# Two attention and two feed-forward layers on one core: tile statistics issued one tile ahead, the first K steps on two transposed chunks, the fourth tile transposed by DMA, the denominator's halves stacked in one operand

## The chip, the core and the metric

The kernel runs on one core of a Trainium2 chip (trn2). The metric is the device time of one execution in microseconds (us); lower is better. One profiled execution gives the rows that are quoted here. Its engines are named as in the profile: PE (TensorE matmuls), PEld (TensorE weight loads), DVE (VectorE), ACT (ScalarE), POOL (GpSimd) and SP (SyncE, which here only issues DMAs).

## The reference

x has 2048 rows of 1024 bf16 numbers. Four layers follow each other, attention and feed-forward in turn, each with a layer norm and a residual. Cut to what matters:

```python
def _A_ref(x, wqkv, wo):              # linear attention, 32 heads of 32
    q, k, v = split(x @ wqkv)
    phi = lambda t: jnp.where(t > 0, t + 1, jnp.exp(t)) + 1e-6
    pq, pk = phi(q), phi(k)
    kv = jnp.einsum("bhsd,bhse->bhde", pk, v)
    z = jnp.einsum("bhsd->bhd", pk)                       # sum over all rows
    num = jnp.einsum("bhqd,bhde->bhqe", pq, kv)
    den = jnp.einsum("bhqd,bhd->bhq", pq, z)[..., None] + 1e-6
    return merge(num / den) @ wo

def _B_ref(x, w_gate, w_up, w_down):  # width 3584
    return ((x @ w_gate) * (x @ w_up)) @ w_down

x = x + _A_ref(_layernorm(x), ...); x = x + _B_ref(_layernorm(x), ...)
x = x + _A_ref(_layernorm(x), ...); x = x + _B_ref(_layernorm(x), ...)
```

## The kernel before

The 2048 rows are 16 tiles of 128 rows; four tiles are a group. x stays in SBUF (`X`). The order of instructions on each engine is the order in which the kernel's code calls them: there is no scheduler, and each engine works through its own list and waits where a semaphore is not there yet. All DMAs are issued by SP, in the order of the code. They use eight semaphores in turn, so that the ninth DMA is issued only when the first has landed, and so on.

**Layer A** (attention, `layer_A`, L221) goes through these stages.

- *Norm and transpose.* `ln_stats(t)` (L180) takes mean and variance of a tile on DVE (two statistics instructions, L183, and an aggregate, L185) and has POOL form rstd, the inverse standard deviation (L187, L189). `ln_apply(t)` (L192, row L194) writes the normalized tile `XN`. `turn` (L197) transposes a tile into `xT` by DMA; `norm(t)` (L337) is all three.
- *The first group of the first layer* is different (L348 to L399). Nothing is there to be computed while x comes in, so the first tiles are only centred (`centre`, L349, x minus mean), and PE transposes them by multiplying with an identity (`turn_pe`, L354, eight 128x128 chunks into one PSUM tile). ACT copies chunks 0 to 3 to `xT` (L361), DVE chunks 4 to 7 (`turn_rest`, L363, row L364). The factor rstd is applied later, as a scale of the activations. The mean of tile 1 comes from ACT (L372). `idle(n)` (L172) are n matmuls on zeros. `k_part(t, a, b)` (L230) does the steps a to b of the K product of tile t, two 128x512 matmuls for each step (`both`, L202, row L204); step k needs row block k of the K weights, which come in eight DMAs of 256 KB.
- *K and Q.* `k_unit` and `q_unit` are 16 matmuls each. `phi` (L206) follows: ACT makes exp and relu (L209, L210), DVE finishes (L213, L214). `weave` puts one DVE job of the list `fill` after each unit of the list `main`. In the first layer these are the norm steps of the tiles 4 to 15 and then `zs`, additions of finished K tiles to the f32 accumulator `zacc` (`z_unit`, L255, row L258).
- *z.* `zacc` holds one sum for each partition. `z_split` (L261) divides it into two bf16 halves: the rounded value (L262) and the rest (L263). `z_sum` (L265) multiplies both with a matrix of ones, which adds up the 128 partitions and puts the sum on all of them, and ACT copies it back to `zacc` (L269).
- *Products.* `g_unit(m)` (L286) is 32 matmuls over all tiles of `XN` and K; the 31st needs K of tile 15. ACT copies its result (L291). `kv_unit(m)` (L296) is eight 128x128 matmuls (L301). `div_unit(t)` (L271) divides Q by the denominator on DVE (L276 to L282) and has it transposed by DMA. `q_with_m` (L310) and `out_unit` (L328) end the layer. L423 to L428 give the order: two g units, then `z_sum`, `kv_unit(0)`, and so on.

**Layer B** (feed-forward) is `gu_unit` (L452) and `d_unit` (L472) for each group. For the very last tile, `d_end` (L481) replaces `d_unit`: it cuts the 1024 output columns into pieces of 512, 256 and 256, with 28 matmuls for each; every piece is added to `X` (L468) and stored (L470).

PSUM gives three buffers to the tag `mm` (1024 f32 a partition) and one to `kv`.

Of the kernel before, what the change touches and what calls it, by code (L numbers as in the profile page):

```python
# [9 lines left out]
ALU = mybir.AluOpType  # L10
AX = mybir.AxisListType
BF16 = mybir.dt.bfloat16
F32 = mybir.dt.float32
# [13 lines left out]
def kernel(  # L27
# [11 lines left out]
    nc = tc.nc  # L39
    P = 128  # L40
    S, D = A_x.shape[1], A_x.shape[2]
    F = B_w_gate.shape[1]
    NT = S // P
    KD = D // P
# [3 lines left out]
    TPG = G // P  # L48
# [7 lines left out]
    small = ctx.enter_context(tc.tile_pool(name="small", bufs=4))  # L56
    psum = ctx.enter_context(tc.tile_pool(name="psum", bufs=1, space=bass.MemoryType.PSUM))
# [10 lines left out]
    xT = [const.tile([P, KD, G], BF16, tag=f"xT{i}", name=f"xT{i}") for i in range(NG)]  # L68
# [4 lines left out]
    W3 = const.tile([P, 4 * D], BF16, tag="W3", name="W3")  # L73
    KVb = const.tile([P, KD, P], BF16, tag="KVb", name="KVb")

    def rows(ap, n):
        return ap.rearrange("p (t n) -> p t n", n=n)
# [6 lines left out]
    wo = [W3[:, c * D:(c + 1) * D] for c in range(4)] + [PQ[1][:, c * D:(c + 1) * D] for c in range(4)]  # L84
    pq = [PQ[0][:, i * D:(i + 1) * D] for i in range(4)] + [PQ[1][:, i * D:(i + 1) * D] for i in range(4)]
    zacc = GL[:, 0:2 * D].bitcast(F32)
    zhl = rows(W3[:, 0:2 * D], D)
    Gs = [GL[:, (2 + i) * D:(3 + i) * D] for i in range(2)]
    ring = [rows(R2[:, i * KD * NB:(i + 1) * KD * NB], NB) for i in range(4)]
    ring += [rows(W1[:, i * KD * NB:(i + 1) * KD * NB], NB) for i in range(2)]  # L90
# [18 lines left out]
    def load_x(t):  # L109
        load(X[:, t, :], x_view[:, t, :])  # L110

    def load_k(a, b):
        load(wkv[:, a:b, :], wqkv_v[:, a:b, D:2 * D])
# [5 lines left out]
    def load_q():  # L119
        for a in (0, 4):  # L120
            load(wq[:, a:a + 4, :], wqkv_v[:, a:a + 4, 0:D])
# [12 lines left out]
    for c in range(2):  # L134
        load(X[:, 0, c * NB:(c + 1) * NB], x_view[:, 0, c * NB:(c + 1) * NB])
    load_x(1)
    load_k(0, 1)
    load_x(2)
    for k in range(1, 4):
        load_k(k, k + 1)  # L140
    load_x(3)
    for k in range(4, 8):
        load_k(k, k + 1)
    load_q()
    for t in range(4, NT):
        load_x(t)

    ident = const.tile([P, P], BF16, tag="ident", name="ident")  # L150
# [3 lines left out]
    ones = const.tile([P, P], BF16, tag="ones", name="ones")  # L154
# [17 lines left out]
    def idle(n):  # L172
        for _ in range(n):
            nc.tensor.matmul(out=zps[:, 0, :], lhsT=xT[3][:, 0, 0:P], rhs=xT[3][:, 0, :], start=True, stop=True)
# [5 lines left out]
    def ln_stats(t):  # L180
        st = small.tile([P, 2, 6], F32, tag="st", name="st")
        for c in range(2):
            nc.vector.bn_stats(out=st[:, c, :], in_=X[:, t, c * NB:(c + 1) * NB])  # L183
        mv = small.tile([P, 2], F32, tag="mv", bufs=NT, name="mv")
        nc.vector.bn_aggr(out=mv[:], in_=st[:])  # L185
        ve = small.tile([P, 1], F32, tag="ve", name="ve")
        nc.gpsimd.tensor_scalar(out=ve[:], in0=mv[:, 1:2], scalar1=1e-5, scalar2=None, op0=ALU.add)  # L187
        rstd = small.tile([P, 1], F32, tag="rstd", bufs=NT, name="rstd")
        nc.gpsimd.tensor_tensor(out=rstd[:], in0=ve[:], in1=mhalf[:], op=ALU.pow)  # L189
        stat[t] = (mv, rstd)  # L190

    def ln_apply(t, dst):  # L192
        mv, rstd = stat[t]
        nc.vector.tensor_scalar(out=dst, in0=X[:, t, :], scalar1=mv[:, 0:1], scalar2=rstd[:],  # L194
                                op0=ALU.subtract, op1=ALU.mult)

    def turn(src, slot, tl):  # L197
        nc.sync.dma_start_transpose(out=xT[slot][:, :, tl * P:(tl + 1) * P], in_=src)
# [3 lines left out]
    def both(ps, lhsT, rhs, start, stop):  # L202
        for n in range(2):
            nc.tensor.matmul(out=ps[:, n, :], lhsT=lhsT, rhs=rhs[:, n * NB:(n + 1) * NB], start=start, stop=stop)  # L204
# [16 lines left out]
    def layer_A(li):  # L221
# [8 lines left out]
        def k_part(t, a, b):  # L230
            if a == 0:
                open_ps[t] = mm_tile()
            ps = open_ps[t]
            tl = t % TPG
            for k in range(a, b):
                both(ps, xT[t // TPG][:, k, tl * P:(tl + 1) * P], wkv[:, k, :], k == 0, k == KD - 1)
            if b == KD:
                phi(ps, PK[:, t, :], scale_of(t))
# [20 lines left out]
            return run  # L259

        def z_split():  # L261
            nc.vector.tensor_copy(out=zhl[:, 0, :], in_=zacc)  # L262
            nc.vector.tensor_tensor(out=zhl[:, 1, :], in0=zacc, in1=zhl[:, 0, :], op=ALU.subtract)  # L263

        def z_sum():  # L265
            ps = mm_tile()
            for h in range(2):
                both(ps, ones[:], zhl[:, h, :], h == 0, h == 1)
            nc.scalar.copy(out=zacc, in_=flat(ps))  # L269

        def div_unit(t):  # L271
# [65 lines left out]
        def norm(t, stats=True):  # L337
            def run():
                if stats:
                    ln_stats(t)  # L340
                ln_apply(t, XN[:, t, :])
                turn(XN[:, t, :], t // TPG, t % TPG)
            return run

        def zs(*ts):
            return lambda: [z_unit(t)() for t in ts]

        if first:  # L348
            def centre(t, mean):  # L349
                nc.vector.tensor_scalar(out=XN[:, t, :], in0=X[:, t, :], scalar1=mean, scalar2=None, op0=ALU.subtract)  # L350

            pts = {}

            def turn_pe(t):  # L354
                if t == 1:
                    pts[t] = psum.tile([P, KD, P], BF16, tag="mm", bufs=3, name="pt1")
                else:
                    pts[t] = psum.tile([P, KD, P], BF16, tag="kv", bufs=1, name="pt")
                for k in range(KD):
                    nc.tensor.transpose(out=pts[t][:, k, :], in_=XN[:, t, k * P:(k + 1) * P], identity=ident[:])  # L360
                nc.scalar.copy(out=xT[0][:, 0:4, t * P:(t + 1) * P], in_=pts[t][:, 0:4, :])  # L361

            def turn_rest(t):  # L363
                nc.vector.tensor_copy(out=xT[0][:, 4:8, t * P:(t + 1) * P], in_=pts[t][:, 4:8, :])  # L364

            mean1 = small.tile([P, 1], F32, tag="mean1", bufs=1, name="mean1")
            junk = small.tile([P, D], BF16, tag="eb", bufs=3, name="junk")

            idle(9)
            ln_stats(0)  # L370
            centre(0, stat[0][0][:, 0:1])
            nc.scalar.activation(out=junk[:], in_=X[:, 1, :], func=ACT.Copy, scale=1.0 / D, accum_out=mean1[:])  # L372
            turn_pe(0)
            idle(1)
            centre(1, mean1[:])
            turn_pe(1)
            ln_stats(2)
            centre(2, stat[2][0][:, 0:1])
            turn_rest(0)
            turn_rest(1)  # L380
            for t in range(2):
                k_part(t, 0, 2)
            for t in range(2):
                k_part(t, 2, 3)
            turn_pe(2)
            for t in range(2):
                k_part(t, 3, 4)
            ln_stats(3)
            centre(3, stat[3][0][:, 0:1])
            turn_rest(2)  # L390
            ln_stats(1)
            k_part(2, 0, 4)
            turn_pe(3)
            turn_rest(3)
            for t in range(3):
                k_part(t, 4, 8)
            k_part(3, 0, 8)
            for t in range(TPG):
                ln_apply(t, XN[:, t, :])  # L399
            main = [q_unit(t) for t in range(4)] + [k_unit(t) for t in range(4, 8)] + [q_unit(t) for t in range(4, 8)]  # L400
            main += [k_unit(t) for t in range(8, 16)]
            fill = [norm(t) for t in range(4, 16)]
            fill += [zs(1, 2), zs(3, 4), zs(5, 6), zs(7), zs(8), zs(9), zs(10, 11), zs(12)]
            do(weave(main, fill))
            do([zs(13, 14, 15), z_split])
        else:
            main = [k_unit(t) for t in range(4)] + [q_unit(t) for t in range(4)]
            main += [k_unit(t) for t in range(4, 8)] + [q_unit(t) for t in range(4, 8)]
            main += [k_unit(t) for t in range(8, 16)]
            fill = [norm(t, False) for t in range(12, 16)]  # L410
            fill += [zs(1), zs(2), zs(3)] + [lambda: None] * 2
            fill += [zs(4), zs(5), zs(6), zs(7)] + [lambda: None] * 3 + [zs(8), zs(9), zs(10), zs(11)]
            do(weave(main, fill))
            do([zs(12, 13, 14, 15), z_split])
# [66 lines left out]
    def d_end(t):  # L481
        def run():
            tl = t % TPG
            for a, b in ((0, 512), (512, 768), (768, 1024)):
                ps = mm_tile()
                for f in range(KF):
                    nc.tensor.matmul(out=ps[:, 0, 0:b - a], lhsT=hT[:, f, tl * P:(tl + 1) * P], rhs=wd[f][:, a:b],  # L487
                                     start=(f == 0), stop=(f == KF - 1))
                add_store(t, a, b, ps[:, 0, 0:b - a], True)
        return run  # L490

    def do(units):
        for u in units:
            u()
# [80 lines left out]
```

## Time and profile before

| What | Value |
|---|---|
| median of 4 runs | 1633.5 us (1633.14 to 1633.61) |
| profiled execution, whole | 1633.54 us |
| its span, first to last instruction | 1631.6 us |
| TensorE clock granted | full from 5.8 us on; half before |
| x and weights, first 20 us | the DMA engines are about full (window 7 to 13 us: 390 GB/s) |
| first K matmul, first g matmul, first z_sum matmul of the first layer | 7.06, 91.67, 105.97 us |
| first z_sum matmul of the third layer | 915.45 us |
| last addition starts, last store issued | 1628.49, 1628.94 us |

A row of the timeline has the start, the length, the engine, the line of the code, the operation, the output and the inputs, their shapes, and a count where equal instructions were merged. In brackets stands how long the engine was idle before, and what ended it. The end of a matmul is modelled, so that rows of matmuls overlap a little; their starts are exact. About one matmul record in 50 is missing from the trace, which shows as one step of 0.43 us instead of 0.216.

### The profile page before, as it was taken

Reading aid. Unit: us, or ns where it says so; the run is one execution under the profiler, and the core shown is the slowest. Engines: PE = TensorE matmul, PEld = TensorE weight load, DVE = VectorE, ACT = ScalarE, POOL = GpSimd, SP = SyncE. Lnnn points to the kernel's source line nnn. Section 1 sums busy time; section 2 is a strip of 40 time slices with the busy share of each in tenths; the row PEclk is TensorE's granted clock in tenths of the full one; section 3 lists DMA queues with packets and bytes.
Section 4 is the critical chain, followed back from the end, with each engine's and each line's share of the span. In section 5 each row is a group of like instructions: output and inputs, shape, how many; then the busy total and the mean of one; then the engine's idle time right before and its main releaser. Section 6 shows DMA issues by size and latency. Waiting matters only on the chain.

```text
span 1631.6 us, 17617 instructions
## 1 busy us (share of the span) xinstructions
PE 1617.9 (99%) x7510; PEld 743.2 (46%) x7662; DVE 608.4 (37%) x889; ACT 287.3 (18%) x386; POOL 53.8 (3%) x141
## 2 busy tenths in 40 slices
PE   9999999999999999999999999999999999999999
PEld 4444444444444444444444444444444444444444
DVE  6799853211311221243245698432123113211111
ACT  5523201100110110011045222011011101101110
POOL 1100000000000000010000000000000000000000
PEclk9999999999999999999999999999999999999999
DMA  6324755521550453142420258555236405522400
GB/s 219 65 65 110 232 161 163 160 64 52 146 189 1 123 163 102 51 150 65 89 60 1 78 103 232 155 175 161 65 90 175 142 20 171 165 65 65 155 0 27
DMA packets 234686, 182.56 MB, mean 112 GB/s; under 512 B 100080, under 2 KB 215408, under 8 KB 234608
## 3 DMA queue, kind: packets, MB, share of 16 engines
q1 hardware_dynamic: 234608, 181.43, 38.4%
q8 instruction: 60, 0.98, 0.3%
q14 instruction: 18, 0.15, 0.0%
HBM read 153.09 MB, written 4.19 MB: 96 GB/s over the span
## 4 chain that ended last, share of the span: by engine, by line
PE 95%; DVE 2%; issue 1%; DMA 1%; POOL 0%; SPq 0%; ACT 0%; DVEq 0%
PE ps L460 47%; PE ps L204 47%; DVE GL L258 1%; PE ps L487 1%; DVE st L183 1%; PE kv L301 0%; DVE R L214 0%; DMA X<-in_A_x_dram 0%; DVE e L213 0%; DVE PQ L214 0%; PE pm L204 0%; POOL rstd L189 0%; SPq L107 0%; DVE R L194 0%; DMA xT<-R 0%
## 5 line engine op out<-in xcount | busy, mean ns | idle before, releaser
L460 PE MATMUL ps<-xT,R 128*128 128x512 bf16 x2382 | 525.9, 379 | 2.7
L460 PEld LDWEIGHTS <-R 128*128 128x128 bf16 x2432 | 238.0, 98 | 286.9
L464 DVE TENSOR_TENSOR R<-gs,ps 128x512 bf16<-128x512 f32 x224 | 154.1, 688 | 533.3 <-ACT gs L463 533.3
L204 PEld LDWEIGHTS <-R 128*128 128x128 bf16 x2248 | 219.8, 98 | 264.8 <-issue 0.6
L463 ACT COPY gs<-ps 128x512 f32<-128x512 f32 x224 | 131.4, 586 | 1039.1 <-PE ps L460 1013.3
L460 PE MATMUL ps<-xT,W 128*128 128x512 bf16 x1130 | 250.1, 379 | 1.1
L204 PEld LDWEIGHTS <-xT 128*128 128x128 bf16 x1536 | 149.4, 98 | 178.8 <-DMA xT<-R 1.5
L204 PE MATMUL ps<-W,xT 128*128 128x512 bf16 x1001 | 225.1, 379 | 1.7 <-DMA xT<-R 0.6
L460 PEld LDWEIGHTS <-W 128*128 128x128 bf16 x1152 | 112.7, 98 | 135.9
L204 PE MATMUL ps<-W,R 128*128 128x512 bf16 x730 | 169.3, 379 | 0.7
L468 DVE TENSOR_TENSOR X<-X,ps 128x1024 bf16<-128x1024 bf16 (+2 forms) x34 | 39.4, 1159 | 335.9 <-PE ps L204 304.4
L204 PE MATMUL ps<-R,R 128*128 128x512 bf16 x501 | 112.4, 379 | 1.0 <-DVE R L214 0.3
L204 PE MATMUL ps<-PQ,R 128*128 128x512 bf16 x487 | 111.3, 379 | 0.5
L204 PE MATMUL ps<-R,xT 128*128 128x512 bf16 x502 | 110.3, 379 | 0.5
L209 ACT ACTIVATE e<-ps 128x1024 bf16<-128x1024 f32 x56 | 57.4, 1025 | 146.3 <-PE ps L204 90.7
L183 DVE BATCH_NORM_STATS2 st<-X 128x6 f32<-128x512 bf16 x128 | 81.9, 682 | 2.2 <-DMA X<-in_A_x_dram 2.1
L187 POOL TENSOR_SCALAR ve<-mv 128x1 f32<-128x1 f32 x64 | 15.4, 241 | 1337.4 <-DVE mv L185 1337.4
L204 PE MATMUL ps<-GL,R 128*128 128x512 bf16 x242 | 58.1, 379 | 0.4
L204 PE MATMUL ps<-xT,R 128*128 128x512 bf16 x242 | 57.9, 379 | 0.3
L334 DVE TENSOR_TENSOR X<-X,ps 128x1024 bf16<-128x1024 bf16 x32 | 38.8, 1213 | 28.0 <-PE ps L204 27.2
L194 DVE TENSOR_SCALAR R<-X,mv,rstd 128x1024 bf16<-128x1024 bf16 x64 | 33.7, 543 | 36.0 <-POOL rstd L189 36.0
L213 DVE TENSOR_SCALAR e<-e 128x1024 bf16<-128x1024 bf16 x64 | 27.1, 424 | 43.1 <-ACT e L209 43.1
(62 smaller groups left out, 461.0 us busy)
## 6 DMA issues: line engine op xcount, KB each, us to landing
R<-in_B_w_gate_dram SPq DMA_DIRECT2D x38, 1024.0 KB, 5.5
R<-in_B_w_up_dram SPq DMA_DIRECT2D x38, 1024.0 KB, 7.6
W<-in_B_w_gate_dram SPq DMA_DIRECT2D x18, 1024.0 KB, 5.4
W<-in_B_w_up_dram SPq DMA_DIRECT2D x18, 1024.0 KB, 7.3
W<-in_A_wqkv_dram SPq DMA_DIRECT2D x10, 1024.0 KB, 6.6
W<-in_B_w_down_dram SPq DMA_DIRECT2D x6, 1024.0 KB, 11.4
PQ<-in_B_w_down_dram SPq DMA_DIRECT2D x4, 1024.0 KB, 8.0
X<-in_A_x_dram SPq DMA_DIRECT2D x15, 256.0 KB, 6.6
```

The source lines that it names most:

```text
L183: nc.vector.bn_stats(out=st[:, c, :], in_=X[:, t, c * NB:(c + 1) * NB])
L194: nc.vector.tensor_scalar(out=dst, in0=X[:, t, :], scalar1=mv[:, 0:1], scalar2=rstd[:], op0=ALU.subtract, op1=ALU.mult)
L204: nc.tensor.matmul(out=ps[:, n, :], lhsT=lhsT, rhs=rhs[:, n * NB:(n + 1) * NB], start=start, stop=stop)
L209: nc.scalar.activation(out=e[:], in_=flat(ps), func=ACT.Exp, **sc)
L213: nc.vector.tensor_scalar(out=e[:], in0=e[:], scalar1=1.0, scalar2=EPS, op0=ALU.min, op1=ALU.add)
L258: nc.vector.tensor_tensor(out=zacc, in0=in0, in1=PK[:, t, :], op=ALU.add)
L334: nc.vector.tensor_tensor(out=X[:, t, :], in0=X[:, t, :], in1=flat(ps), op=ALU.add)
L460: nc.tensor.matmul(out=ps[:, n, :], lhsT=w[:, k, j * P:(j + 1) * P], rhs=xT[g % 2][:, k, :], start=(k == 0), stop=(k == KD - 1))
L463: nc.scalar.copy(out=gs[:], in_=ps[:, 0, :])
L464: nc.vector.tensor_tensor(out=hT[:, f, :], in0=gs[:], in1=ps[:, 1, :], op=ALU.mult)
L468: nc.vector.tensor_tensor(out=X[:, t, a:b], in0=X[:, t, a:b], in1=ps, op=ALU.add)
L487: nc.tensor.matmul(out=ps[:, 0, 0:b - a], lhsT=hT[:, f, tl * P:(tl + 1) * P], rhs=wd[f][:, a:b], start=(f == 0), stop=(f == KF - 1))
```

## The change

It has four parts.

1. **Statistics a tile ahead.** In the first layer, the norm step of a tile (`norm_step`) now applies the statistics that were taken one step earlier, and then takes those of the next tile. The applies of the tiles 0 to 3 stand no longer in front of the Q units but with the z additions of the K units 8 to 11 (`xn_and_z`); the z additions are dealt out in another way.
2. **The opening.** Tile 0 is transposed in two PSUM tiles: chunks 0 and 1, which DVE copies, and 2 to 7, which ACT copies. The K steps 0 and 1 of tile 0 follow at once, ahead of the transposes of tile 1. Tile 1 is split 4 and 4, tile 2 is copied by ACT in one piece. Tile 3 is transposed by DMA. One idle matmul is left out. The second block of K weights is loaded ahead of x tile 2; the Q weights and x tiles 4 to 15 are issued behind the DMA transpose of tile 3.
3. **Stacked halves.** `z_split` first folds the partitions 64 to 127 of `zacc` onto 0 to 63 (an ACT copy and a DVE addition), and then puts the rounded value on the partitions 0 to 63 of one operand and the rest on 64 to 127. `z_sum` is one pass of two matmuls. Both attention layers use it.
4. **Last tile.** The pieces are 512, 384 and 128 columns.

```diff
-    zhl = rows(W3[:, 0:2 * D], D)
+    zhl = W3[:, 0:D]
...
     load_x(1)
-    load_k(0, 1)
+    for k in range(2):
+        load_k(k, k + 1)
     load_x(2)
-    for k in range(1, 4):
+    for k in range(2, 4):
         load_k(k, k + 1)
     load_x(3)
     for k in range(4, 8):
         load_k(k, k + 1)
-    load_q()
-    for t in range(4, NT):
-        load_x(t)
...
         def z_split():
-            nc.vector.tensor_copy(out=zhl[:, 0, :], in_=zacc)
-            nc.vector.tensor_tensor(out=zhl[:, 1, :], in0=zacc, in1=zhl[:, 0, :], op=ALU.subtract)
+            up = small.tile([P, D], F32, tag="tmp", bufs=1, name="up")
+            nc.scalar.copy(out=up[0:64, :], in_=zacc[64:P, :])
+            nc.vector.tensor_tensor(out=zacc[0:64, :], in0=zacc[0:64, :], in1=up[0:64, :], op=ALU.add)
+            nc.vector.tensor_copy(out=zhl[0:64, :], in_=zacc[0:64, :])
+            nc.vector.tensor_tensor(out=zhl[64:P, :], in0=zacc[0:64, :], in1=zhl[0:64, :], op=ALU.subtract)
 
         def z_sum():
             ps = mm_tile()
-            for h in range(2):
-                both(ps, ones[:], zhl[:, h, :], h == 0, h == 1)
+            both(ps, ones[:], zhl, True, True)
             nc.scalar.copy(out=zacc, in_=flat(ps))
...
-            def turn_pe(t):
...
+            def turn_pe(t, cut):
+                for h, (i, j) in enumerate(((0, cut), (cut, KD))):
+                    if i == j:
+                        continue
+                    tag, bufs = ("mm", 3) if h else ("kv", 1)
+                    pt = psum.tile([P, KD, P], BF16, tag=tag, bufs=bufs, name="pt")
+                    pts[t, h] = pt
+                    for k in range(i, j):
+                        nc.tensor.transpose(out=pt[:, k, :], in_=XN[:, t, k * P:(k + 1) * P], identity=ident[:])
+
+            def take(copy, t, h, a, b):
+                copy(out=xT[0][:, a:b, t * P:(t + 1) * P], in_=pts[t, h][:, a:b, :])
...
-            turn_pe(0)
-            idle(1)
+            turn_pe(0, 2)
+            take(nc.vector.tensor_copy, 0, 0, 0, 2)
+            take(nc.scalar.copy, 0, 1, 2, 8)
             centre(1, mean1[:])
-            turn_pe(1)
+            k_part(0, 0, 2)
+            turn_pe(1, 4)
+            take(nc.vector.tensor_copy, 1, 0, 0, 4)
+            take(nc.scalar.copy, 1, 1, 4, 8)
             ln_stats(2)
             centre(2, stat[2][0][:, 0:1])
-            turn_rest(0)
-            turn_rest(1)
-            for t in range(2):
-                k_part(t, 0, 2)
-            for t in range(2):
-                k_part(t, 2, 3)
-            turn_pe(2)
+            k_part(0, 2, 3)
+            k_part(1, 0, 3)
             for t in range(2):
                 k_part(t, 3, 4)
+            turn_pe(2, 8)
+            take(nc.scalar.copy, 2, 0, 0, 8)
             ln_stats(3)
             centre(3, stat[3][0][:, 0:1])
-            turn_rest(2)
+            turn(XN[:, 3, :], 0, 3)
+            load_q()
+            for t in range(4, NT):
+                load_x(t)
             ln_stats(1)
-            k_part(2, 0, 4)
-            turn_pe(3)
-            turn_rest(3)
-            for t in range(3):
-                k_part(t, 4, 8)
+            for t in range(2):
+                k_part(t, 4, 6)
+            k_part(0, 6, 8)
+            k_part(2, 0, 6)
+            for t in range(1, 3):
+                k_part(t, 6, 8)
             k_part(3, 0, 8)
-            for t in range(TPG):
-                ln_apply(t, XN[:, t, :])
+            ln_stats(4)
+
+            def norm_step(t):
+                def run():
+                    norm(t, False)()
+                    if t + 1 < NT:
+                        ln_stats(t + 1)
+                return run
+
+            def xn_and_z(t, *ts):
+                return lambda: [ln_apply(t, XN[:, t, :])] + [z_unit(u)() for u in ts]
...
-            fill = [norm(t) for t in range(4, 16)]
-            fill += [zs(1, 2), zs(3, 4), zs(5, 6), zs(7), zs(8), zs(9), zs(10, 11), zs(12)]
+            fill = [norm_step(t) for t in range(4, 16)]
+            fill += [xn_and_z(0, 1), xn_and_z(1, 2), xn_and_z(2, 3), xn_and_z(3, 4), zs(5, 6), zs(7, 8), zs(9, 10),
+                     zs(11, 12)]
...
-            for a, b in ((0, 512), (512, 768), (768, 1024)):
+            for a, b in ((0, 512), (512, 896), (896, 1024)):
```

More of the change, by code (lines that the diff above doesn't have):

```diff
@@ L352, in layer_A @@
             pts = {}
-            def turn_pe(t):
[L355 to L364, printed above, removed]
+            def turn_pe(t, cut):
[9 more added lines that the diff above has]
+                copy(out=xT[0][:, a:b, t * P:(t + 1) * P], in_=pts[t, h][:, a:b, :])
             mean1 = small.tile([P, 1], F32, tag="mean1", bufs=1, name="mean1")
```

## The prediction

> **What bounds the kernel now.** I read the page's busy shares and its chain of waits first, to see which engine the end hangs on.
>
> ```profile
> PE 1617.9 (99%) x7510; PEld 743.2 (46%) x7662; DVE 608.4 (37%) x889; ACT 287.3 (18%) x386; POOL 53.8 (3%) x141
> PE 95%; DVE 2%; issue 1%; DMA 1%; POOL 0%; SPq 0%; ACT 0%; DVEq 0%
> ```
>
> TensorE is the bound. A busy share of 99% does not say what is left, because matmul ends are modelled; starts do. In the timeline 128x512 matmuls start 0.216 us apart (the chain's pieces of 49 begin every 10.79 us, 49 plus one record missing). So I went through the starts for larger steps. After the first K matmul at 7.06 us there are few: 0.10 at 42.6, 0.72 at 46.8, 0.49 at 98.6, about 0.2 twice around 176 to 178 and the same pair near 986. Everything this change can win lies there, before 7.06, in matmuls dropped, and behind the last matmul. The stretches in question, TensorE alone:
>
> ```profile
> 4.98 1.02 PE L360 MATMUL pt<-ident,R 128*128 128x128 bf16 x8
> 5.84 0.38 PE L174 MATMUL ps<-xT 128*128 128x512 bf16 x1
> 6.60 0.62 PE L360 MATMUL pt<-ident,R 128*128 128x128 bf16 x8 [0.38 <-DVE R L350]
> 7.06 2.75 PE L204 MATMUL ps<-W,xT 128*128 128x512 bf16 x12
> ...
> 44.76 1.46 PE L204 MATMUL ps<-W,xT 128*128 128x512 bf16 x6
> 46.77 1.47 PE L204 MATMUL ps<-W,xT 128*128 128x512 bf16 x6 [0.55 <-DMA xT<-R]
> ...
> 91.67 6.64 PE L204 MATMUL ps<-R,R 128*128 128x512 bf16 x29
> 98.64 7.50 PE L204 MATMUL ps<-R,R 128*128 128x512 bf16 x34 [0.33 <-DVE R L214]
> 105.97 0.38 PE L204 MATMUL ps<-W,ones 128*128 128x512 bf16 x1
> ```
>
> At 46.77: six starts from 44.76 end at 45.84, the next is 0.93 later, 0.72 too much. At 98.64: 30 matmuls from 91.67 (29 records, one missing) take 6.48, so 0.49 is lost. Both are VectorE's doing, as the timeline of that engine shows:
>
> ```profile
> 43.05 0.55 DVE L194 TENSOR_SCALAR R<-X,mv,rstd 128x1024 bf16<-128x1024 bf16 x1 [1.00 <-POOL rstd L189]
> ...
> 98.50 5.00 DVE L258 TENSOR_TENSOR GL<-GL,R 128x1024 f32<-128x1024 f32 x4
> ...
> 103.53 0.69 DVE L262 CAST W<-GL 128x1024 bf16<-128x1024 f32 x1
> 104.26 1.23 DVE L263 TENSOR_TENSOR W<-GL,W 128x1024 bf16<-128x1024 f32 x1
> ```
>
> Each of the twelve norm steps makes VectorE stand 1.00 us for POOL's rstd. Its step is 4.12 us (31.28, 35.40, 39.51, 43.63 are the transposes' issues), TensorE's unit 16 x 0.216 = 3.45. VectorE drifts back, until a transpose lands (46.72) as it is wanted.
>
> **Part 1, statistics a tile ahead.** A norm step becomes apply then next statistics. From the starts: 0.52 (L213) + 0.61 (L214) + 0.46 (L194) + 1.31 + 0.24 (L183, L185) = 3.14, under 3.45, with POOL's 0.9 us beside VectorE's next phi. VectorE keeps pace with TensorE, and transposes land about 3.6 us ahead of their K units: k_unit(4) is wanted at 35.5; its tile is applied at 28.2 (q_unit(0) ends at 25.2, its phi 2.8 later as near 16 to 18 us), issued at 28.8, landed 3.1 later at 31.9. The waits of 0.10 and 0.72 go: **-0.82**. The four applies move to the K units 8 to 11, whose VectorE step is 0.52 + 0.61 + 0.46 + 1.14 (L258) = 2.73: hidden. From k_unit(12) on, with two adds, a step is 3.53 as at 80.50 to 84.03, 0.08 slower than TensorE's, so phi of tile 15 ends near 93.9 where g_unit(0) wants it at 97.2: the 0.49 goes too, **-0.49**.
>
> **Part 2, the opening.** Removed from TensorE: one idle matmul and eight transposes (0.44 after 7.06). The first K matmuls can start at 5.9: two chunks turned by 5.2, a 256-column copy (0.42 for 512, so some 0.28) done by 5.7, k row 0 landed at 5.8 (2.11 + 3.7). K row 1 takes the place of x tile 2 in the queue and lands where that did, 6.8. TensorE still runs at half speed there (idle matmuls 0.43 apart, transposes 0.107 until 5.84, 0.055 from 6.60); a rise of the clock as late as 8 us would cost nothing, since row 2 is awaited anyway. Four matmuls and the turn of tile 1 end at 7.7. But then comes k_part(0,2,3), and row 2, still seventh in the queue, lands at 8.3 (3.53 + 4.8). Before, eight matmuls lay before row 2; now four do, since tile 1 waits behind. TensorE stands 0.6 us. From 8.34: 60 matmuls (12.95) and the turn of tile 2 (0.44) give the end of K at 21.73; before, from 7.06: 64 (13.81) and 0.88, 21.76. So **-0.03**. Bounds: -0.7 if row 2 is early, +0.9 if k1 and k2 are each half a microsecond late.
>
> Other ends of it: tile 2's statistics start at 8.1 (before 6.79) behind the copy for tile 1, centre(2) ends at 10.2, wanted at 10.9; its one ACT copy of 1024 columns ends at 12.7, wanted at 14.0. Centre(3) ends at 12.2, the DMA transpose is issued then (1.23 of SP's time) and lands at 15.4, wanted at 18.3. Behind it on SP stand load_q and twelve x loads; before they were issued from 7.40 on. Two 1 MB halves at the 390 GB/s of the window 7 to 13 land near 17 and 20, wanted at 21.7 and 23.4; x tile 4 near 20.5, wanted at 24.6, the others 0.7 apart against 3.45. All hidden, with 3 us or more; without that cover each late microsecond would be TensorE's.
>
> **Part 3, stacked halves.** z_sum has two matmuls instead of four, in two layers: 4 x 0.216 = **-0.86**. The price is a longer z_split: an ACT copy of 64x1024 f32 (no such row; between 1.02, L269 from PSUM, and 1.06, L372 from SBUF; I take 1.05), an add (1.23 as L263), the cast (0.69), the subtract (1.23); on 64 partitions as long as on 128, because the free size is the same. With handovers 4.33 from the last add to the operand, before 1.99. Layer 0: five adds from 93.78 (1.26 each) end at 100.03; the operand is ready at 104.4. TensorE, from 90.77 with two g units of 6.91, wants it at 104.58. Just hidden, **0**; every further 0.1 us past the first 0.18 counts in full. Layer 2: adds end at 909.4, ready at 913.8, wanted at 915.45 (its row starts there): hidden. ScalarE's copy of g_unit(0) is now queued behind the wait for the adds and ends near 102; kv_unit(0) wants it at 105. Later stages don't give the gain back: the divisions begin after ACT's zacc copy, which waits for the copy of g_unit(1), so they move with TensorE, and VectorE has 2.0 us of idle before phi at 173.4. The waits near 176 and 178 stay: KVb hangs on q_unit(13), TensorE's own.
>
> **Part 4, last tile.** The third cut shrinks from 256 to 128 columns, and so does what follows the last matmul:
>
> ```profile
> 1622.38 0.69 DVE L468 TENSOR_TENSOR X<-X,ps 128x512 bf16<-128x512 bf16 x1 [4.82 <-PE ps L487]
> 1625.44 0.42 DVE L468 TENSOR_TENSOR X<-X,ps 128x256 bf16<-128x256 bf16 x1 [2.37 <-PE ps L487]
> 1628.49 0.42 DVE L468 TENSOR_TENSOR X<-X,ps 128x256 bf16<-128x256 bf16 x1 [2.63 <-PE ps L487]
> ```
>
> 0.69 to 0.42 for half the columns, so 0.28 for 128: -0.14. Stores land 2.0, 1.7 and 1.6 us after issue for 256, 128 and 64 KB, so 32 KB saves at most 0.1. Against it stand two rules of the Trainium skill. "DMA: Bandwidth & Descriptors" (Specifications) says that under 512 B the engine reads, modifies and writes; the rows now have 256 B. No store here is that narrow; the fixed 1.5 us dominates, so I take -0.06 and keep +0.3. "TensorE: Matmul & The Clock Gate" (Back-to-back issue gap) gives 81 ns for a sustained 128-wide pair of weight load and matmul, where the row of kv_unit has eight in 0.44 us (106.84 to 107.28), 55 ns. By the row the 28 matmuls take 1.54 and the cuts together 12.15, as before (12.16); by the rule 2.27, +0.73. The run of eight is short, but it has the same pairs, and 56 pairs of 256 hold 109: I take the row.
>
> **The sum.** -0.82 - 0.49 - 0.03 - 0.86 - 0.20 = -2.40. The profiled execution took 1633.54 (span 1631.6, 1.94 around it), the median of the runs is 1633.5. With 0.1 for the edge in part 3: **1631.2 us**, 0.14% less. About 0.2% (3.3 us) is what a measurement can tell from no change.
>
> **The rivals.**
> - *z_split becomes the bound* (slower). Place: z_sum's first matmul. For: 0.18 us of margin. The split's stall is its delay less 0.18 in layer 0 and less 1.65 in layer 2, so from 2.1 us late (4.3 becoming 6.4) the gain of 2.4 is gone; if the cross-partition steps take double, 4.15 + 2.68 come on top: **1638**. Against: the rows of both engines go by free size. Chance 0.06.
> - *The gain is eaten later*: TensorE, 1.8 us earlier, meets a transfer or VectorE in the division stage. For: VectorE is 80 to 96% busy from 100 to 180. Against: its idle before 173.4, and no step in TensorE's starts from 107 to 174. Only z_sum and the tail would stay: **1632.7**. 0.10.
> - *The last tile by the rules*: +0.73 + 0.3, **1632.2**. 0.10.
> - *The opening gives more*: row 2 lands as TensorE comes to it, and the tail gives its 0.3: **1630.2**. 0.12.
> - The forecast, 1630.5 to 1631.9: 0.62.
>
> **How the numbers follow.** The range 1630.0 to 1632.9 holds the forecast, the opening's bound below and the two small rivals above, and leaves out z_split and half of the edges. Faster by over 0.2% (under 1630.2) takes the better half of the fourth rival and a little beside it: 0.11. Slower by over 0.2% is z_split beyond 5.7 us of loss, or an early load that I have wrong: 0.06. The rest, 0.83, is within.
>
> **What would show it.** Right: no POOL wait before L194's rows and no TensorE step at 42 to 47; g_unit(0) without a wait; two matmuls on ones; K matmuls from 5.9, then a wait for W near 8.3; z_sum starting within 0.3 us of the last g matmul; 28 matmuls in 1.5 us at the end. Wrong: a gap before the ones matmuls, the last 28 in over 2 us, or a first q_unit that waits for W.

## The result, and the profile after

The changed kernel takes 1630.87 us (median of 40 runs, 1630.14 to 1632.54); beside it the kernel before takes 1633.4 us (median of 60 runs, 1632.86 to 1635.23). The ratio is 0.9985, with a 95% interval from 0.998 to 0.9989: about 2.5 us less. The profiled execution took 1631.16 us where that of before took 1633.54; its span is 1629.1 us.

The page after, its busy shares and the chain that ended last:

```profile
PE 1615.7 (99%) x7498; PEld 741.0 (45%) x7649; DVE 609.6 (37%) x889; ACT 289.3 (18%) x387; POOL 55.2 (3%) x141
PE 99%; issue 1%; DMA 0%; SPq 0%; DVE 0%; another core or an unknown queue 0%
```

Both lines say that TensorE still bounds the kernel. The chain's share of TensorE rose from 95 to 99%, and VectorE's 2% are gone from it. The busy times hardly move, so again the starts tell more. TensorE in the opening (start, length, engine, line, operation, count):

```profile
5.04 0.62 PE L365 MATMUL pt<-ident,R 128*128 128x128 bf16 x8
5.71 1.19 PE L202 MATMUL ps<-W,xT 128*128 128x512 bf16 x4
6.73 0.61 PE L365 MATMUL pt<-ident,R 128*128 128x128 bf16 x8
8.30 2.75 PE L202 MATMUL ps<-W,xT 128*128 128x512 bf16 x12 [0.96 <-DMA W<-in_A_wqkv_dram]
```

K work begins at 5.71 instead of 7.06, but only four matmuls of it fit before TensorE waits for the third block of K weights, until 8.30. The norm steps, on VectorE:

```profile
28.11 0.54 DVE L192 TENSOR_SCALAR R<-X,mv,rstd 128x1024 bf16<-128x1024 bf16 x1
...
31.56 0.54 DVE L192 TENSOR_SCALAR R<-X,mv,rstd 128x1024 bf16<-128x1024 bf16 x1
...
35.01 0.54 DVE L192 TENSOR_SCALAR R<-X,mv,rstd 128x1024 bf16<-128x1024 bf16 x1
```

The bracket with 1.00 us for POOL's rstd is gone, and the steps are 3.45 us apart, as TensorE's units are. From the g units to the denominator:

```profile
90.76 13.98 PE L202 MATMUL ps<-R,R 128*128 128x512 bf16 x63
...
93.76 6.26 DVE L256 TENSOR_TENSOR GL<-GL,R 128x1024 f32<-128x1024 f32 x5
100.05 1.04 ACT L263 COPY up<-GL 64x1024 f32<-64x1024 f32 x1 [7.16 <-DVE GL L256]
...
101.13 1.22 DVE L264 TENSOR_TENSOR GL<-GL,up 64x1024 f32<-64x1024 f32 x1 [1.11 <-ACT up L263]
102.38 0.68 DVE L265 CAST W<-GL 64x1024 bf16<-64x1024 f32 x1
103.10 1.22 DVE L266 TENSOR_TENSOR W<-GL,W 64x1024 bf16<-64x1024 f32 x1
...
104.57 0.59 PE L202 MATMUL ps<-W,ones 128*128 128x512 bf16 x2
```

The two g units run as one piece (63 records), with no wait inside. The operand of `z_sum` is finished at 103.10 + 1.22 = 104.32, and the matmul follows the last g matmul. Nothing is lost there, by a narrow margin.

The starts of both executions side by side, with what the prediction's terms add up to at that place:

| Place | before | after | difference | predicted |
|---|---|---|---|---|
| first g matmul | 91.67 | 90.76 | -0.91 | -0.85 |
| first z_sum matmul, first layer | 105.97 | 104.57 | -1.40 | -1.34 |
| first z_sum matmul, third layer | 915.45 | 913.61 | -1.84 | -1.77 |
| last addition | 1628.49 | 1626.23 | -2.26 | -2.20 |
| end of the span | 1631.6 | 1629.1 | -2.5 | -2.40 |

The gain is complete by 110 us but for one pair of matmuls in the third layer and the last 0.2 us. Between those places nothing is given back.

### The profile page after: what moved, and what is told of

Same layout as the page of the kernel before. It is cut to its first block, busy times and chain, and to the rows that moved or that the text cites. A ratio compares the mean times of both kernels' runs of the same rounds, so it can differ in the third digit from the quotient of the medians.

```text
span 1629.1 us, 17583 instructions
## 1 busy us (share of the span) xinstructions
PE 1615.7 (99%) x7498; PEld 741.0 (45%) x7649; DVE 609.6 (37%) x889; ACT 289.3 (18%) x387; POOL 55.2 (3%) x141
## 4 chain that ended last, share of the span: by engine, by line
PE 99%; issue 1%; DMA 0%; SPq 0%; DVE 0%; another core or an unknown queue 0%
PE ps L202 50%; PE ps L480 47%; PE ps L507 1%; PE kv L303 0%; DMA W<-in_A_wqkv_dram 0%; PE pm L202 0%; SPq L107 0%; PE pt L365 0%; DVE X L488 0%
## 5 line engine op out<-in xcount | busy, mean ns | idle before, releaser
L488 DVE TENSOR_TENSOR X<-X,ps 128x1024 bf16<-128x1024 bf16 (+3 forms) x34 | 39.4, 1159 | 335.7 <-PE ps L202 326.0
```

Source lines behind the costliest of these rows:

```text
L488: nc.vector.tensor_tensor(out=X[:, t, a:b], in0=X[:, t, a:b], in1=ps, op=ALU.add)
```

## Experiments: each part alone

The first four kernels each have one part of the change in the kernel before, whose median beside them was 1633.64 us.

**Part 1 alone.** Only the norm steps and the z additions are those of the changed kernel:

```diff
-            fill = [norm(t) for t in range(4, 16)]
+            fill = [norm_step(t) for t in range(4, 16)]
...
+            fill += [xn_and_z(0, 1), xn_and_z(1, 2), xn_and_z(2, 3), xn_and_z(3, 4), zs(5, 6), zs(7, 8), zs(9, 10),
+                     zs(11, 12)]
```

> The kernel before with part 1 alone (norm steps with the statistics a tile ahead, applies of tiles 0 to 3 and the z additions dealt out as in the change). Theory: the waits at 42.6 and 46.8 us (0.10 + 0.72) and the one in g_unit(0) (0.49) are gone, nothing else moves: 1.3 us less, about 1632.1, and no step in TensorE's starts between 7.1 and 105 us. Rival, the gain is made elsewhere or is eaten in the division stage: under 0.4 us less.

Measured: 1632.0 us (1631.71 to 1632.64), ratio 0.999 (0.9982 to 0.9999); the profiled execution took 1632.24, 1.30 less than that of before. TensorE in it:

```profile
39.73 10.52 PE L204 MATMUL ps<-W,xT 128*128 128x512 bf16 x47
...
90.88 13.98 PE L204 MATMUL ps<-R,R 128*128 128x512 bf16 x63
104.70 1.03 PE L204 MATMUL ps<-W,ones 128*128 128x512 bf16 x4
```

One piece runs across 42 to 47 us, where before there were two breaks, and the g units are one piece too. `z_sum` starts 1.27 us earlier than before. So this part takes away both stalls, and it is more than half of the whole gain. Which of its pieces (statistics ahead, applies moved, additions dealt out anew) removes which stall was not tried one by one; the row without POOL's bracket speaks for the first at the stalls of 42 to 47 us.

**Part 2 alone.** The loads and the first K steps are as changed, all the rest as before.

```diff
-            turn_pe(0)
-            idle(1)
+            turn_pe(0, 2)
+            take(nc.vector.tensor_copy, 0, 0, 0, 2)
+            take(nc.scalar.copy, 0, 1, 2, 8)
...
+            k_part(0, 0, 2)
+            turn_pe(1, 4)
```

> The kernel before with part 2 alone (order of loads, two early chunks, fourth tile by DMA). Theory: row block 2 of the K weights lands at 8.3 us whatever is done before, and 60 matmuls and one turn follow it as 64 matmuls and two turns followed 7.06: within 0.15 us of before, about 1633.4, K ends at 21.7. Rival, the early K matmuls bring the whole opening forward: 0.5 to 1.2 us less.

Measured: 1633.3 us (1632.6 to 1635.27), ratio 0.9998 (0.9989 to 1.0007). That cannot be told from no change. Its timeline shows the waits that part 1 removes still in place, under other line numbers:

```profile
7.79 2.75 PE L202 MATMUL ps<-W,xT 128*128 128x512 bf16 x12 [0.28 <-DMA W<-in_A_wqkv_dram]
...
46.10 6.22 PE L202 MATMUL ps<-W,xT 128*128 128x512 bf16 x28 [0.47 <-DMA xT<-R]
...
98.00 7.50 PE L202 MATMUL ps<-R,R 128*128 128x512 bf16 x33 [0.35 <-DVE R L212]
```

In this execution the third K block landed at 7.75 us, half a microsecond sooner than in the executions of before (8.3) and after (8.26), and the K work followed it 0.04 us later, as in the execution after. When that block comes decides the opening, not how soon the first four matmuls are done.

**Part 3 alone.** `z_split` and `z_sum` as changed.

```diff
-            for h in range(2):
-                both(ps, ones[:], zhl[:, h, :], h == 0, h == 1)
+            both(ps, ones[:], zhl, True, True)
```

> The kernel before with part 3 alone (stacked halves, longer z_split), so that VectorE is late in the first layer. Theory: the split is 2.34 us longer; in the first layer the operand is ready near 107.8 and wanted at 105.98, a wait of 1.8 us against 0.43 saved; in the third layer it is hidden and 0.43 is saved: 1.0 us more than before, about 1634.4. Rival, the split is hidden in both layers without part 1 as well: 0.86 less, 1632.5.

Measured: 1634.41 us (1633.97 to 1634.69), ratio 1.0003 (0.9995 to 1.0012): the median is 0.77 us *above* the one beside it, with four matmuls less. The interval does not exclude no change; the timeline shows the loss:

```profile
98.28 5.00 DVE L258 TENSOR_TENSOR GL<-GL,R 128x1024 f32<-128x1024 f32 x4
...
106.36 1.22 DVE L268 TENSOR_TENSOR W<-GL,W 64x1024 bf16<-64x1024 f32 x1
...
107.73 0.59 PE L204 MATMUL ps<-W,ones 128*128 128x512 bf16 x2 [1.81 <-DVE W L268]
```

Here the z additions are those of before: the last four end at 103.28, three microseconds later than with part 1. The longer split ends at 107.58, and TensorE, through with its g matmuls, stands: the step to the first matmul on ones is 2.19 us where 0.216 would be normal, 1.97 lost. With two matmuls saved in each layer, 1.97 - 0.86 = +1.1 comes out; the first g unit was 0.2 earlier by the opening, which leaves the +0.9 of the spans (1632.5 against 1631.6). In the third layer the operand is ready in time, as was worked out. So part 3 is a gain of 0.86 only behind part 1, and alone a loss.

**Part 4 alone.**

```diff
-            for a, b in ((0, 512), (512, 768), (768, 1024)):
+            for a, b in ((0, 512), (512, 896), (896, 1024)):
```

> The kernel before with part 4 alone (cuts 512, 384, 128). Theory: matmuls go at 55 ns, the last addition is 0.14 shorter and the store a little: 0.2 us less, about 1633.2. Rival, pairs of 128 go at 81 ns and stores of 256 B rows are slower: 0.7 to 1.0 us more.

Measured: 1633.05 us (1632.58 to 1633.7), ratio 0.9997 (0.9988 to 1.0005). It is not slower, and some tenths faster at best: the opening of the profiled execution happened to start its K work at 6.69 instead of 7.06, so that of its 0.6 us (span 1631.0) about 0.35 is not the tail's. The tail by itself: from the start of the last addition to the end of the span there are 2.88 us, where the kernel before has 3.10.

## Experiments: the margins, and what is left

These start from the changed kernel. They ran in two sets, each with the kernel before beside it. The first set has the lengthened split, the other K order, the put-off `phi` and the cut of 64 columns (kernel before: 1633.65 us). The second has the other three and the changed kernel, unaltered, for comparison (kernel before: 1633.51 us). Across the sets, a kernel is compared by its distance to the kernel before, which is 2.72 us for the unaltered one:

> The changed kernel once more, beside the next two, because their differences are smaller than what separates two sets of runs. All theories: 1630.6 to 1631.1 us, in the opening a wait for row block 2 of the K weights whose end is where that block lands (7.75 to 8.8 in the profiles so far).

Measured: 1630.79 us (1630.42 to 1631.48), ratio 0.9984 (0.9975 to 0.9993).

**The split made 1.4 us longer.** Two copies of the accumulator onto itself stand in front of the fold, in both attention layers.

```diff
             up = small.tile([P, D], F32, tag="tmp", bufs=1, name="up")
+            for _ in range(2):
+                nc.vector.tensor_copy(out=zacc, in_=zacc)
             nc.scalar.copy(out=up[0:64, :], in_=zacc[64:P, :])
```

> The changed kernel with two copies of zacc onto itself in front of the split, in both layers (the sums are the same). Their rows give the delay, 1.4 to 2.5 us. Theory: the operand has 0.2 us to spare in the first layer and 1.7 in the third, so the wait is delay less 0.2 in the first layer and delay less 1.7 or nothing in the third: 1.2 to 3 us more than the changed kernel. Rival, later stages absorb such a wait (or the gain was never bound to z_sum): no more than 0.5 us.

Measured: 1632.29 us (1631.79 to 1632.87), ratio 0.9992 (0.9983 to 1.0001): 1.36 below the kernel before where the unaltered one is 2.72 below, so a loss of about 1.4.

```profile
104.22 1.22 DVE L268 TENSOR_TENSOR W<-GL,W 64x1024 bf16<-64x1024 f32 x1
...
105.58 0.59 PE L202 MATMUL ps<-W,ones 128*128 128x512 bf16 x2 [1.19 <-ACT GL L295]
```

The bracket blames ACT's copy of a g unit; the true releaser is VectorE, whose row ends at 105.44, 0.14 before the matmul. The copies take 1.42 us and delay the operand by 1.45; TensorE lost 1.35 here, and nothing in the third layer. The delay comes through to the end of the kernel: its span is 1.0 us longer although its opening was 0.34 faster. So the margin of `z_split` in the first layer is about 0.1 us, and the division stage behind it absorbs nothing.

**K steps of tile 1 ahead of the third block.** TensorE had room before 8.30. The steps 0 and 1 of tile 1 need only blocks that are there:

```diff
-            k_part(0, 2, 3)
-            k_part(1, 0, 3)
+            k_part(1, 0, 2)
+            for t in range(2):
+                k_part(t, 2, 3)
```

> The changed kernel with K steps 0 and 1 of tile 1 in front of step 2 of tile 0, so that TensorE has four matmuls while row block 2 is on its way. Theory: the wait of 0.96 us before 8.3 shrinks to about 0.3 us (until the copy of tile 1 is done, near 7.6): K ends 0.65 earlier, 0.65 us less than the changed kernel, about 1630.2. Rival, later row blocks (k3 at 8.9, k4 at 10.2, k7 at 12.2) or the Q weights (18.8 and 21.5) take over as the wait: under 0.2 us less.

Measured: 1630.9 us (1630.48 to 1631.6), ratio 0.9983 (0.9975 to 0.9992). A miss: the medians show no gain.

```profile
7.04 0.61 PE L365 MATMUL pt<-ident,R 128*128 128x128 bf16 x8
7.95 2.76 PE L202 MATMUL ps<-W,xT 128*128 128x512 bf16 x12 [0.30 <-DVE xT L368]
```

In this execution it is the copy of tile 1 that TensorE waits for. The tile is turned only behind the four matmuls of tile 0, and its copy comes after that. But the loads of this execution came late: the second half of x tile 0 landed at 3.95 us (3.50 in the execution after) and the third K block at 8.78. Even so the K work went on at 7.95, 0.35 sooner than after. So the trace shows a new wait, but not why the medians of 11 runs show no gain. That stays open.

**The turn of tile 1 drawn forward as well.** It goes between the K steps 0 and 1 of tile 0, so that its copy runs beside two matmuls:

```diff
-            k_part(0, 0, 2)
+            k_part(0, 0, 1)
             turn_pe(1, 4)
+            k_part(0, 1, 2)
```

with the order of the experiment before.

> The changed kernel with the turn of tile 1 between K steps 0 and 1 of tile 0, and K steps 0 and 1 of tile 1 in front of step 2 of both: TensorE has eight matmuls and two turns to do while row block 2 comes. Theory: the wait for row block 2 is gone, K ends 0.6 to 0.8 us earlier: about 1630.2, at least 0.4 below the control. Rival, seen in the run with the other K order: the opening is bound by the later row blocks or by the landing of x and the Q weights, the wait only moves: within 0.2 us of the control. The trace tells which landing the K matmuls wait for.

Measured: 1630.35 us (1630.03 to 1630.7), ratio 0.998 (0.9971 to 0.9989), 0.44 under the unaltered kernel of the same batch.

```profile
5.76 0.60 PE L202 MATMUL ps<-W,xT 128*128 128x512 bf16 x2
6.33 0.62 PE L365 MATMUL pt<-ident,R 128*128 128x128 bf16 x8
6.79 1.50 PE L202 MATMUL ps<-W,xT 128*128 128x512 bf16 x6
8.73 1.89 PE L202 MATMUL ps<-W,xT 128*128 128x512 bf16 x8 [0.45 <-DMA W<-in_A_wqkv_dram]
```

Eight K matmuls lie before the third block, as in the kernel before, and 56 behind it instead of 60: 4 x 0.216 = 0.86 at most. In this execution the block landed as late as 8.69, so that TensorE still stood for 0.45 with its eight done; the medians show about half of the 0.86. So it is confirmed in direction, at the lower end of the size expected, that the four matmuls behind the block cost the opening its gain.

**The step near 176 us.** `q_with_m` begins with products of `KVb`, which wait for ACT work queued behind a `phi`. The end of that `phi` was put off:

```diff
-        q[6] = q_unit(14, later)
+        q[5], q[6] = q_unit(13, later), q_unit(14, later)
```

> The changed kernel with the VectorE end of q_unit(13)'s phi put off into q_with_m, so that the masking of KVb no longer stands behind it. Theory: KVb is ready before TensorE comes to it and the step of 0.22 us at 174.4 and its twin near 983 go: 0.4 us less than the changed kernel, about 1630.5. Rival: the put-off work delays the copies of M, and the time comes back there: no change.

Measured: 1630.81 us (1630.2 to 1632.17), ratio 0.9983 (0.9974 to 0.9992). Not to be told from the unaltered kernel. In the profile the step at 174.3 is gone, but one has come up where `out_unit(0)` begins:

```profile
180.96 0.59 PE L202 MATMUL ps<-W,xT 128*128 128x512 bf16 x2
181.52 2.75 PE L202 MATMUL ps<-R,xT 128*128 128x512 bf16 x12
```

0.56 us from start to start where two matmuls take 0.43: 0.13 given back, in both attention layers.

**Both together**, with the put-off end of `phi` now behind the first product's copy instead of the third step:

```diff
+                if c == 0:
+                    do(early)
...
+        q[5], q[6] = q_unit(13, early), q_unit(14, later)
```

> The run before it with KVb in front as well: the VectorE end of q_unit(13)'s phi comes behind the first copy of M, that of q_unit(14) stays where it was. Theory: the step of 0.22 at the first M matmul goes in both layers and no step comes back at out_unit(0) (as 0.13 did when both ends were put off to the same place): 0.4 us less than the run before it, the fastest of all. Rival: nothing, because the copies of M come late instead.

Measured: 1629.96 us (1629.43 to 1630.65), ratio 0.9979 (0.997 to 0.9988): 0.39 below the experiment with the opening alone (whose runs overlap with these), 0.83 below the unaltered kernel, and the fastest of all. `out_unit(0)` has no step before it now:

```profile
179.69 0.59 PE L202 MATMUL ps<-W,xT 128*128 128x512 bf16 x2
180.12 6.21 PE L202 MATMUL ps<-R,xT 128*128 128x512 bf16 x28
```

One step of 0.18 stays, at 174.94 and again at 983.75.

**A last cut of 64 columns**, which tests what bounds the tail:

```diff
-            for a, b in ((0, 512), (512, 896), (896, 1024)):
+            for a, b in ((0, 512), (512, 960), (960, 1024)):
```

> The changed kernel with cuts of 512, 448 and 64. If a pair of weight load and matmul is bound by the columns alone, 28 pairs of 64 take 0.8 us, the sum of the cuts stays, and the end comes 0.1 us earlier. If the weight load bounds it (55 ns as for 128), they take 1.5 us and the end comes 0.6 to 0.7 later; if a pair costs 81 ns, 1.4 later. The trace's last 28 starts tell it.

Measured: 1630.82 us (1630.49 to 1632.39), ratio 0.9984 (0.9975 to 0.9993), the same as with 128.

```profile
1625.12 0.40 PE L507 MATMUL ps<-PQ,R 128*128 128x64 bf16 x8
1625.36 0.40 PE L507 MATMUL ps<-W,R 128*128 128x64 bf16 x8
1625.59 0.28 PE L507 MATMUL ps<-GL,R 128*128 128x64 bf16 x4
```

Eight pairs of weight load and matmul start every 0.24 us, 29 ns a pair. Even here the columns set the pace and the weight loads stay hidden, so that the cuts together take the same time whatever the last one's width. The last addition is shorter (0.22 against 0.29), which is too little for the total to show.

**Q weights behind all x tiles**, which tests whether the late loads are covered:

```diff
             turn(XN[:, 3, :], 0, 3)
-            load_q()
             for t in range(4, NT):
                 load_x(t)
+            load_q()
```

> The changed kernel with the Q weights loaded behind the x tiles 4 to 15. Theory: the move of load_q costs nothing only because of the 3 us of cover; here the halves land near 26.5 and 29.3, wanted at 21.5 and 23.2, and TensorE stands 5 to 6 us, none of which comes back: 1636 to 1637. Rival, the later stages take up such a delay: under 2 us more.

Measured: 1639.19 us (1639.01 to 1639.89), ratio 1.0037 (1.0022 to 1.0052), 8.4 above the unaltered kernel and more than expected. The timeline names the wait, and the table of windows (busy time and count of PE, PEld, DVE, ACT and POOL, then the granted clock, the DMA share and GB/s) has the rest:

```profile
27.32 6.91 PE L202 MATMUL ps<-W,xT 128*128 128x512 bf16 x21 [5.91 <-DMA W<-in_A_wqkv_dram]
```

```profile
21.00:24.00 3.00, 0.42 (x2) 0.00 (x0) 1.51 (x3) 2.45 (x3) 0.00 (x0) 1.00 1.04 391
24.00:27.00 3.00, 0.00 (x0) 0.00 (x0) 1.70 (x4) 0.00 (x0) 0.79 (x2) 0.67 1.05 395
27.00:29.00 2.00, 1.68 (x5) 0.59 (x6) 0.00 (x0) 0.00 (x0) 0.00 (x0) 0.50 1.00 364
29.00:31.00 2.00, 2.00 (x6) 0.72 (x5) 0.00 (x0) 0.00 (x0) 0.00 (x0) 0.50 0.04 13
31.00:32.00 1.00, 1.00 (x4) 0.38 (x3) 0.00 (x0) 0.00 (x0) 0.00 (x0) 0.57 0.00 0
32.00:33.00 1.00, 1.00 (x7) 0.41 (x6) 0.00 (x0) 0.00 (x0) 0.00 (x0) 1.00 0.00 0
```

The first half of the Q weights landed at 27.19, and TensorE lost 6.07 us between two starts. During that wait its clock went down to 0.50, and it stayed there for some 4.5 us of work after it: starts are 0.427 us apart until 31.54. Nine such steps, 0.21 too long each, and one of 0.16 too long at either edge make the remaining 2.2 us. The Trainium skill, "TensorE: Matmul & The Clock Gate" (What's actually happening), has the clock halved after an idle window of about 3.4 us and full again after as long a busy one, with windows that run freely; the table agrees, with a drop some 3.6 us after the last matmul (a mean of 0.67 over 24 to 27 us is a third at 1.0) and 4.5 us to come back. The cover was real; without it, a late microsecond cost more than one here.

## Why the prediction was right, point by point

The forecast of 1631.2 us was made against the profiled execution, and the profiled execution after took 1631.16. The median of the 40 runs is 0.3 lower and lies in the range as well. That the two profiled executions agree so closely is partly luck: the block that the opening waits for landed at 8.30 before and at 8.26 after, and in the other profiled executions, of all kernels, anywhere between 7.62 and 8.78. By the steps:

- **Part 1, -1.31.** Right in place and size: the profiled execution with this part alone is 1.30 shorter, and `z_sum` starts 1.27 earlier in it. The medians differ by 1.6, with 0.9 between the highest and lowest of the 11 runs. The interval ends at 0.9999, just short of no change, so the vanished breaks are the stronger evidence. The first transpose was worked out to land at 31.9 and landed at 31.76.
- **Part 2, -0.03.** Right in the profiled execution, and for the reason given: TensorE waits for the third K block, which landed at 8.26 where 8.3 was taken. The medians of part 2 alone (0.34 less, the interval spanning no change) are too coarse to tell -0.03 from a few tenths. TensorE stood 0.96 us where 0.6 was worked out, because the first two K blocks came sooner (5.41 and 6.26 for 5.8 and 6.8) and because the transposes of tile 0 ran at full pace, not at half (eight in 0.62 us); this changed nothing behind the block. Not seen was how much the landing varies from run to run (below). The covers were right in kind but **mis-sized**: the Q halves were to land near 17 and 20 and landed at 18.75 and 21.46; x tile 4 at 22.13 instead of 20.5. The term that failed is the rate: 390 GB/s was taken for these loads from their issue on. What the DMA queues moved from 11 to 17 us, in GB/s for 40 slices of 0.15 us:

```profile
GB/s 301 109 14 27 27 0 0 0 0 0 0 0 24 195 225 220 212 205 200 189 191 82 46 14 205 82 191 27 177 177 314 396 396 423 423 396 437 355 355 382
```

  From 11.3 to 12.8 almost nothing moves, while SP holds back the loads for the transpose of tile 3. Up to 15.5 the rate is 225 or less, with mostly the transpose's small packets in it (1071 of the 1457 packets in that window are under 512 B), and only then the loads run at about 390. So the second Q half, wanted at 23.4, had 1.9 us of cover where 3.4 were counted. It did no harm, but it can come close: in the profile of the unaltered kernel run again, the half landed at 23.07, and the first matmul that uses it started at 23.30. The experiment with the Q weights last shows what a miss would cost.
- **Part 3, -0.86.** Right, and so was the edge: the operand was to be ready at 104.4 and wanted at 104.58; it was ready at 104.32 and used at 104.57. A handover of 0.14 lies between the end of the row and the matmul (0.15 and 0.14 in the two experiments with a stall), so the true slack is about 0.11, which the lengthened split confirms. The estimate for the copy (1.05) was 1.04, and the other three rows of 64 partitions are as long as those of 128. Two sums are off by 0.05: 91.67 less 0.85 is 90.82, not 90.77, and five additions of 1.26 from 93.78 end at 100.08, not 100.03. Both err the same way, so that the margin stays about 0.2; the 0.1 set aside for this edge was not needed. What the prediction left unsaid is how far this part leans on part 1: with the additions of before it is a loss.
- **Part 4, -0.20.** From the start of the last addition to the end of the span there are 2.88 us instead of 3.10 (unrounded times): -0.22. The addition takes 0.29 (0.28 worked out). The two rules that the prediction set against it did not bear out. The last cut:

```profile
1624.46 0.61 PE L507 MATMUL ps<-PQ,R 128*128 128x128 bf16 x8
1624.91 0.61 PE L507 MATMUL ps<-W,R 128*128 128x128 bf16 x8
1625.36 0.39 PE L507 MATMUL ps<-GL,R 128*128 128x128 bf16 x4
1625.58 0.39 PE L507 MATMUL ps<-W,R 128*128 128x128 bf16 x4
1625.81 0.39 PE L507 MATMUL ps<-xT,R 128*128 128x128 bf16 x4
...
1626.23 0.29 DVE L488 TENSOR_TENSOR X<-X,ps 128x128 bf16<-128x128 bf16 x1 [1.01 <-PE ps L507]
```

  24 matmuls start in 1625.81 - 1624.46 = 1.35 us, 56 ns each, where the 81 ns of the Trainium skill, "TensorE: Matmul & The Clock Gate" (Back-to-back issue gap), would need 1.94; the same section's formula for an isolated matmul, columns / 2.4 + 2.5 ns, gives 55.8 and so agrees. The store of 32 KB, with rows of 256 B, landed 1.48 us after its issue and that of 64 KB in the kernel before, with rows of 512 B, 1.58, so that the read-modify-write that the Trainium skill, "DMA: Bandwidth & Descriptors" (Specifications), states for less than 512 B cannot be seen in the time of a store this small.
- **The rivals.** The split as the bound did not happen, but the mechanism is real: with part 1 away, or with 1.4 us more, it decides. The gain eaten later is ruled out by the table of starts: -1.40 at the first `z_sum` is still there, with one pair of matmuls more, 800 us later. (Its price was 0.2 too high: 1633.54 less 0.86 and 0.20 is 1632.5.) The opening that gives more did not come by itself; it took another order of the K steps.

## What to carry to other kernels

When one engine bounds a kernel, compare the starts of its instructions and add up the excess steps: a change can win just those, the work it removes and the tail. Price a part in the order in which it will stand: a split that is hidden behind earlier additions is a loss behind late ones. And when work is moved ahead of an awaited load, count what can really run before it, its own inputs included; here four matmuls that had to stand behind the load took the gain of the opening away, and in another order TensorE waited for the copy of a tile.

## What was not expected of the hardware

- The same load, seventh in the queue and issued at 3.53 or 3.54 us in each kernel looked at, landed between 7.62 and 8.78 us in the executions with a profile. A microsecond of the opening is thus left to chance, and it is as large as most of the effects studied here; the runs of the changed kernel spread over 2.4 us, as do those of the kernel before, so that the landing of this one block need not be the only cause. Where the variation comes from was not tried.
- The clock does not rise at a fixed time either. With the same code up to there, the eight transposes of tile 0 took 0.62 us in the execution after (from 5.04) and 1.03, half the pace, in that with the last cut of 64 columns (from 5.07).
- One wait of 6 us cost 8.3 us of TensorE's time, because of the half clock after it (the experiment with the Q weights last).
- Pairs of a 128x128 weight load and a matmul ran at 29 ns for 64 columns and 56 ns for 128, so that the weight loads cost no time of their own even at 64.
